# Block-sparse attention with an MLP behind it: dense query blocks left out of the sparse tiles, and window copies of the first chunk handed from ScalarE to GpSimd

## The chip, the cores and the metric

The kernel runs on one core of one Trainium2 chip. The metric is the time of one execution in device microseconds (us); the median of three runs of the kernel before is 761.54 us (760.61 to 762.57). A core has a TensorE (PE) for matmuls and transposes, a VectorE (DVE), a ScalarE (ACT), a GpSimd (POOL) and a SyncE (SP). SP and POOL issue nearly all the transfers here, and a transfer that is issued behind a waiting instruction waits with it, because each engine works through its instructions in the order of the program.

## The reference

Queries, keys and values have 4 batches, 8 heads, 768 positions and 64 dimensions. Positions form 24 blocks of 32. A query block sees its own and its two neighbour blocks, the first and the last block, and three sampled blocks; the first and the last query block see everything ("dense" blocks). The result of the attention, 3072 tokens of 512 numbers, goes through two weight matrices with a squared relu between them.

```python
mask = np.abs(blk_i - blk_j) <= window
mask = mask | (blk_i == 0) | (blk_j == 0) | (blk_i == n_blocks - 1) | (blk_j == n_blocks - 1)
for qb in range(n_blocks):
    for kb in sampled_blocks[qb]:
        mask[qb * block:(qb + 1) * block, kb * block:(kb + 1) * block] = True
scores = np.where(mask, scores, -1000000000.0)
...
attn = attn / (np.sum(attn, axis=-1, keepdims=True) + 1e-09)
return np.matmul(attn, v).astype(np.float32)
...
h = np.maximum(x @ w_in, 0.0)          # x 3072x512, w_in 512x2048
return (h * h @ w_out).astype(np.float32)
```

## The kernel before, in words

**Tiles and chunks.** 128 tokens of a batch (four query blocks) are a tile; there are 24 tiles `(b, t)` in `order`, and `k` is a tile's place in it. Three tiles form a chunk of 384 tokens, and there are eight chunks. The MLP of a chunk (`moe(c)`: `hidden` gives `ph` at L788, `project` gives `po` at L816 and L826) runs on PE while the attention of the chunks behind it is worked in between its steps. fp32 products are split into a rounded high part and a low part, and three products are summed, so each weight block has a high part, cast by ACT or DVE, and a low part, subtracted by POOL (`wi`/`wo` at L752 to L755, `WI` at L726 and L727).

**A half.** `Half(b, t, u)` is the attention of four heads of a tile. Each query block needs eight blocks of 32 keys: its window (`kn`, 96 columns) and a gathered set `KG` (first and last block and the three sampled ones, 160 columns). `scores` (L374) writes the scores `s` of the four query blocks into the four groups of 32 partitions: four groups, two column pieces, four heads, 32 matmuls. Then come `maxima` on DVE (L385), exponentials and a turn of the probabilities: for the first six tiles (`MOVED` = 6) by `exps` on ACT (L423), a transposition on PE (`pt`, L437) and copies (`pT`, L446 and L448); for the others by `turn_blocks`, 16 activations `pm` on ACT, each over a square of blocks (L413), and one DVE transposition (L418). `values` (L459) multiplies with the gathered values `V`, again 32 matmuls of 65 columns (64 values and a one for the sum), and `norm` writes `x`. In all this the dense blocks 0 and 23 go along like any other block, although their rows of `x` come from elsewhere.

**A whole.** `Whole(b, pr)` computes the two dense blocks for a pair of heads: scores `g` (L546), exponentials `pg` on ACT (L562), the turned `pTg`, and `pvg` (L604), for which 128 columns of `pTg` (two blocks of two heads) are multiplied in four pieces of 32 columns with each of six tiles of `vn`.

**The values of a tile.** `V[k]` is two tiles per `k`: the first and last block (`static`), a window of three neighbours (`window`) and three sampled blocks. They come by SP's DMAs (`load_static`, `load_window` L304, `load_sampled` L317), save for the second and third tile of the first chunk, whose windows and static blocks are copied from `vn` inside the chip (`copy_window` L217, `copy_static` L209).

**The start.** The first chunk has no MLP beside it. A `Stream` advances in ticks; every fifth tick another unit begins (four wholes, then six halves). Into the ticks go three lists: `fixed`, the copies given to ACT (6 static ones, then the 24 window copies of the third tile, `k` = 2); `moves`, the copies given to DVE (12 for the second half of the second tile); and the cuts. A cut turns a block of the float64 weights to fp32: POOL issues the load `craw` (L692), `AHEAD` = 5 cuts later ACT works on it (L708, L710), one cut later DVE (L719, L720), one later ACT and POOL split it if it stays resident (L726, L727). POOL's own list at the start is written out: gathered keys of two tiles, five loads of weights, 12 window copies, gathered keys of the third tile. `later` holds the key copies of the tiles behind (`copy_keys`, L263), of which a piece is issued at every tick or second tick.

The order on each engine is that of the code (a manual schedule); the pools add the waits.

Of the kernel before, what the change touches and what calls it, by code (L numbers as in the profile page):

```python
# [75 lines left out]
CUT_0 = (30, 5)  # L76
# [6 lines left out]
ON_ACT = 12  # L83
# [13 lines left out]
def tile_block_sparse_attention_moe(ctx: ExitStack, tc, kd, knd, qd, qgd, vd, vnd, samp, const, wcat, out):  # L97
# [59 lines left out]
    V = {0: [one.tile([P, 2, NJ, HW // 2], F32, name=f"V{c}") for c in range(2)]}  # L157
# [33 lines left out]
    def columns(src, us):  # L191

        return src.rearrange("... (u c) -> ... u c", u=2)[..., us, :]

    def load_static(k, u, eng=nc.sync):
        us = halves(k, u)
        if us is None:
            return
        n = 1 if k == 0 else NJ
        for i in range(us.start, us.stop):  # L200
            src = columns(vd[order[k][0], V_STATIC * BLK :], i)
            src = src.unsqueeze(1).broadcast_to([2 * BLK, n, HW // 2])
            eng.dma_start(values_of(k)[0][0 : 2 * BLK, i, 0:n], src)

    def copy_static(k, i, copy):

        src = V[0][0][0 : 2 * BLK, i, 0:1]
        dst = V[k][0][0 : 2 * BLK, i, 1 if k == 0 else 0 :]
        copy(dst, src.broadcast_to(list(dst.shape)))  # L209

    def copy_window(k, i, j, n, copy):
# [5 lines left out]
        copy(V[k][1][(1 + n) * BLK : (2 + n) * BLK, i, j], st["vn", b, i][r : r + BLK, blk // NJ])  # L217

    def load_vn(b, hf, eng=nc.sync, own=None):
# [3 lines left out]
        st["vn", b, hf] = vn  # L223

# [28 lines left out]
    def copy_keys(b, t, own=None):  # L253
# [3 lines left out]
        for u in range(2):  # L257
# [3 lines left out]
            for j in range(NJ):  # L261
# [6 lines left out]
    later = []  # L268

    def load_kg(b, t):  # L270
# [3 lines left out]
        for j in range(NJ):  # L274
# [11 lines left out]
    def load_window(k, u, eng=nc.sync):  # L286
# [5 lines left out]
        runs = []  # L292
        for j in range(NJ):
            c = centre(NJ * t + j)
            if runs and c == runs[-1][-1][1] + 1:
                runs[-1].append((j, c))
            else:
                runs.append([(j, c)])
        for run in runs:
            (j, c), n = run[0], len(run)  # L300
            for i in range(us.start, us.stop):
                src = vd[b, (c - 1) * BLK : (c + 1 + n) * BLK, i * HW // 2 : (i + 1) * HW // 2]
                src = bass.AP(src.tensor, src.offset, [[HW, 3 * BLK], [BLK * HW, n], [1, HW // 2]])
                eng.dma_start(VB[BLK:P, i, j : j + n], src)  # L304

    def load_sampled(k, u, eng, on):
# [6 lines left out]
        v4 = columns(vd[b], us).rearrange("(a p) u c -> p a u c", p=BLK)  # L313
        for j in range(NJ):
            for r in range(NRAND):
                dst = VB[0:BLK, us, j] if r == 2 else VA[(2 + r) * BLK : (3 + r) * BLK, us, j]
                eng.dma_start(dst.unsqueeze(1), v4[:, bass.ds(vals[NRAND * j + r], 1)])  # L317
# [6 lines left out]
    class Half:  # L324


        def __init__(self, b, t, u):
# [3 lines left out]
            self.name = f"{b}_{t}_{u}"  # L331

# [26 lines left out]
        def scores(self):  # L359
# [3 lines left out]
            for i in range(2):  # L363
                pr = 2 * u + i
                for piece in range(2):
                    for j in range(NJ):
                        c = centre(NJ * t + j)
                        for e in range(2):
# [3 lines left out]
                            else:  # L372
                                k, a, z = kg[r, j, :, pr, :], 0, S_WIN
                            nc.tensor.matmul(  # L374
                                self.sb[e][j * BLK : (j + 1) * BLK, i * NSLOT + a : i * NSLOT + z],
# [6 lines left out]
        def maxima(self):  # L382
            m = self.m = rot.tile([P, 2, 2], F32, tag="m", name=f"m{self.name}", bufs=4)
            for e in range(2):
                nc.vector.tensor_reduce(m[:, e], self.sb[e].rearrange("p (i c) -> p i c", i=2), axis=AX, op=ALU.max)  # L385
            self.p = rot.tile([P, 4, 2, NJ, BLK], F32, tag="p", name=f"p{self.name}", bufs=PBUFS)
            if not self.moved:
                nc.vector.tensor_scalar(m, m, -SCALE, None, op0=ALU.mult)
                return
            for e in range(2):  # L390
                nc.vector.tensor_tensor(  # L391
                    self.p[:, 2 * e : 2 * e + 2].rearrange("p h c a s -> p h (c a s)"),
                    self.sb[e].rearrange("p (i c) -> p i c", i=2),
                    m[:, e].unsqueeze(2).broadcast_to([P, 2, NSLOT]),
# [9 lines left out]
        def turn_blocks(self):  # L404
# [4 lines left out]
            for j in range(NJ):  # L409
                if j == 2:  # L410
                    self.next_keys()
                for a in range(NJ):
# [491 lines left out]
    for _ in range(AHEAD):  # L904
        cut_next()
# [107 lines left out]
```

## Time and profile before

| | |
|---|---|
| median of three runs | 761.54 us (760.61 to 762.57) |
| span of the profiled execution | 757.7 us, of which the other 3.8 us of the median lie around it |
| PE busy | 733.0 us (97% of the span) |
| PE weight loads (PEld) | 612.4 us (81%) |
| ACT busy | 539.4 us (71%) |
| POOL busy | 502.1 us (66%) |
| DVE busy | 500.2 us (66%) |
| HBM traffic | 126 GB/s over the span |

The profiled execution has no time of its own beyond its span; the median of the three runs is taken as its time, so that 3.8 us (761.5 less 757.7) lie outside the span. In the span the start (up to about 58 us, before the MLP begins) differs from the rest: there PE is well below full, and ACT, DVE and POOL take turns in a chain of small steps. In the rest PE runs almost without a gap. The views that the prediction shows are windows (busy time of each engine in a stretch), groups (one line and tile: count, busy time, mean of one), and timelines (start, duration, engine, line, operation, count, and in brackets the idle time before with what ended it).

### The profile page before, as it was taken

To read this page: it belongs to the slowest core of one execution; us is meant where nothing else is said; L and a number is where in the kernel's file an instruction comes from. 1 tells how busy PE (TensorE), PEld (TensorE's weight loads), DVE (VectorE), ACT (ScalarE), POOL (GpSimd) and SP (SyncE) were. 2 spreads that over 40 slices of the span, in tenths; PEclk is the share of its full clock that TensorE was granted. 3 is DMA by queue.
4 is the path that set the end of the run, shared out by engine and by line. 5 is a ranking of instruction groups with operands and counts; after the bars stand their busy time and mean duration, and the time that the engine had idled before them with its cause. 6 is when DMAs were issued, how large, how long until landed. Compare 5 with 4: busy or idle time off the path is not lost.

```text
span 757.7 us, 26295 instructions
## 1 busy us (share of the span) xinstructions
PE 733.0 (97%) x9832; PEld 612.4 (81%) x9832; DVE 500.2 (66%) x988; ACT 539.4 (71%) x1193; POOL 502.1 (66%) x636
## 2 busy tenths in 40 slices
PE   5779999999999999999999999999999999999997
PEld 2666777678888888888888888887888888888986
DVE  5785785658785756667777575666868666645452
ACT  5896877898876876689786767679876776733222
POOL 6963844237776675757777567666876575777885
PEclk9899999999999999999999999999999999999999
DMA  8776799644443436544434344654344352201001
GB/s 282 217 210 187 223 272 339 136 119 141 125 119 92 144 90 186 153 105 118 119 102 107 98 126 107 225 120 139 84 122 114 81 138 65 51 1 44 1 1 42
DMA packets 92434, 97.45 MB, mean 129 GB/s; under 512 B 14803, under 2 KB 79700, under 8 KB 92308
## 3 DMA queue, kind: packets, MB, share of 16 engines
q1 hardware_dynamic: 86324, 72.80, 36.6%
q0 software_dynamic: 5696, 22.58, 8.8%
q8 instruction: 78, 1.28, 0.7%
q14 instruction: 48, 0.39, 0.2%
q10 hardware_dynamic: 288, 0.39, 0.1%
HBM read 89.43 MB, written 6.29 MB: 126 GB/s over the span
## 4 chain that ended last, share of the span: by engine, by line
PE 84%; DMA 5%; ACT 5%; DVE 3%; issue 1%; SPq 1%; POOL 1%; ACTq 0%; POOLq 0%; DVEq 0%
PE ph L788 33%; PE po L826 30%; PE s L374 7%; PE pv L459 6%; DMA V<-in_v_dram 3%; PE po L816 3%; PE g L546 2%; PE pvg L604 2%; DMA KG<-in_k_dram 1%; PE pt L437 1%; PE xt L773 1%; DVE xl L777 1%; ACT V L209 1%; DMA kn<-in_kn_dram 1%; SPq L317 1%
## 5 line engine op out<-in xcount | busy, mean ns | idle before, releaser
L413 ACT ACTIVATE pm<-p 32x256 f32<-32x256 f32 x576 | 239.2, 415 | 13.2 <-DVE p L391 4.9
L788 PE MATMUL ph<-xh,wi 128*128 128x384 f32 x832 | 237.8, 347 | 0.0
L826 PE MATMUL po<-wo,gh 128*128 128x512 f32 x672 | 213.8, 399 | 0.0
L755 POOL TENSOR_TENSOR wi<-W,wi 128x512 fp32r<-128x512 f32 x104 | 142.2, 1367 | 66.8 <-DVE wi L754 35.2
L806 POOL TENSOR_TENSOR gl<-gf,gh 128x384 fp32r<-128x384 f32 x112 | 117.4, 1048 | 93.3 <-DVE gf L804 80.9
L755 POOL TENSOR_TENSOR wo<-WO,wo 128x512 fp32r<-128x512 f32 x112 | 145.8, 1301 | 49.5 <-DVE wo L754 48.6
L792 ACT ACTIVATE r<-ph 128x384 f32<-128x384 f32 x128 | 63.0, 492 | 161.6 <-PE ph L788 156.5
L804 DVE SCALAR_TENSOR_TENSOR gf<-ph,r 128x384 f32<-128x384 f32 x112 | 62.3, 556 | 150.7 <-ACT r L792 137.1
L788 PEld LDWEIGHTS ph<-xh,wi 128*128 128x128 f32 x832 | 150.4, 188 | 13.4 <-issue 7.4
L826 PEld LDWEIGHTS po<-wo,gh 128*128 128x128 f32 x672 | 123.5, 188 | 23.0 <-issue 2.8
L788 PE MATMUL ph<-xl,wi 128*128 128x384 f32 x416 | 141.4, 340 | 0.0
L826 PE MATMUL po<-wo,gl 128*128 128x512 f32 x336 | 133.1, 396 | 0.0
L754 DVE CAST wo<-WO 128x512 fp32r<-128x512 f32 x112 | 84.3, 753 | 0.0
L788 PEld LDWEIGHTS ph<-xl,wi 128*128 128x128 f32 x416 | 78.2, 188 | 6.9 <-issue 2.9
L826 PEld LDWEIGHTS po<-wo,gl 128*128 128x128 f32 x336 | 63.1, 188 | 15.7 <-POOL gl L806 1.0
L385 DVE TENSOR_REDUCE m<-s 128x2 f32<-128x512 f32 x96 | 61.6, 683 | 10.6 <-PE s L374 10.2
L799 ACT ACTIVATE gh<-r 128x384 fp32r<-128x384 f32 x112 | 59.0, 527 | 9.3 <-ACT r L792 0.4
L459 PEld LDWEIGHTS pv<-V,pT 128*32 128x32 f32 x3072 | 47.2, 109 | 18.9 <-issue 10.5
L459 PE MATMUL pv<-V,pT 128*32 128x65 f32 x3072 | 56.0, 221 | 4.4 <-ACT pT L446 2.3
L788 PE MATMUL ph<-xh,WI 128*128 128x384 f32 x192 | 54.4, 344 | 0.8 <-ACT xh L776 0.8
L374 PE MATMUL s<-KG,q 64*32 64x160 f32 x1536 | 51.3, 307 | 0.6 <-issue 0.3
L418 DVE STREAM_TRANSPOSE pT<-pm 128x1024 f32<-128x1024 f32 x36 | 44.6, 1238 | 4.9 <-ACT pm L413 4.7
(89 smaller groups left out, 933.9 us busy)
## 6 DMA issues: line engine op xcount, KB each, us to landing
craw<-in_w_dram POOLq DMA_DIRECT2D x32, 512.0 KB, 6.0
V<-in_v_dram SPq DMA_DIRECT2D x504, 32.5 KB, 1.8
KG<-in_k_dram SPq DMA_DIRECT2D x216, 64.0 KB, 2.0
V<-in_v_dram SPq DMA_DIRECT2D x28, 390.0 KB, 4.3
q<-in_q_dram SPq DMA_DIRECT2D x24, 256.0 KB, 3.6
out_dram<-ot SPq DMA_DIRECT2D x22, 256.0 KB, 2.6
V<-in_v_dram SPq DMA_DIRECT2D x16, 292.5 KB, 4.0
vn<-in_vn_dram SPq DMA_DIRECT2D x5, 780.0 KB, 6.2
```

The costliest lines, as they stand in the source:

```text
L374: nc.tensor.matmul(self.sb[e][j * BLK : (j + 1) * BLK, i * NSLOT + a : i * NSLOT + z], q[r, j, pr, :], k, start=True, stop=True,)
L385: nc.vector.tensor_reduce(m[:, e], self.sb[e].rearrange("p (i c) -> p i c", i=2), axis=AX, op=ALU.max)
L413: nc.scalar.activation(p[a * BLK : (a + 1) * BLK, j], x[j * BLK : (j + 1) * BLK, :, a], AF.Exp, scale=SCALE)
L459: nc.tensor.matmul(po[j * BLK : (j + 1) * BLK, h * VW : (h + 1) * VW], self.pT[:, j, 2 * e + i, c], v[:, self.u, j, hv : hv + VW], start=( ...
L754: nc.vector.tensor_copy(w[:, 0], src)
L755: nc.gpsimd.tensor_tensor(w[:, 1], src, w[:, 0], op=ALU.subtract)
L788: nc.tensor.matmul(ph[:, :TOK], w, x, start=(i == 0), stop=(i == len(steps) - 1))
L792: nc.scalar.activation(r, ph[:, :TOK], AF.Relu)
L799: nc.scalar.activation(gh, r, AF.Square)
L804: nc.vector.scalar_tensor_tensor(gf, ph[:, :TOK], 0.0, r, op0=ALU.max, op1=ALU.mult)
L806: nc.gpsimd.tensor_tensor(gl, gf, gh, op=ALU.subtract)
L826: nc.tensor.matmul(acc[c][u], g[:, at], w[:, k], start=(f == 0 and i == 0), stop=(f == NF - 1 and i == 2))
```

## The change

Six edits, in the diff below.

- **Dense blocks left out of the halves.** `groups(t)` lists the query blocks that a half works on: (2, 3, 1) in a batch's first tile, (0, 1, 2) in its last, all four elsewhere. In 16 of the 48 halves `s` and `pv` have 24 matmuls instead of 32, the exponentials and maxima 96 partitions instead of 128, `pm` 12 activations instead of 16, and a quarter of the sampled blocks is neither loaded nor copied. The block at group `g` is no longer block `g` in the first tile, so `norm` writes in two parts there.
- **`pvg` in 64 columns.** The layout of `QG` is changed in the host arrays, so that a head's two dense blocks lie side by side, and `Whole.values` has two pieces of 64 columns instead of four of 32.
- **Halves of `V` side by side.** In the first chunk a row of `V` holds both halves, so one DMA with rows of 2080 bytes brings what two rows of 1040 bytes did, and a window or a static block comes in one DMA.
- **Third tile's windows on POOL.** The 24 copies leave ACT's `fixed` and stand in POOL's list behind the fourth load of weights. That list is now: two loads, 12 window copies, a load, the third tile's keys, a load, 24 window copies, the fifth load.
- **Weights later.** `CUT_0` moves from tick 30 to 35, so five cuts instead of six begin in the first chunk, and the sixth follows in `moe(0)`.
- **Fourth tile's values later.** Its window and sampled loads go to a list `late`, of which one entry is issued every four ticks of `moe(0)`.

```diff
-CUT_0 = (30, 5)
+CUT_0 = (35, 5)
-ON_ACT = 12
+FIRST_LOADS, SECOND_LOADS, THIRD_LOADS = 2, 3, 4
+LATE = (0, 4)
...
-    V = {0: [one.tile([P, 2, NJ, HW // 2], F32, name=f"V{c}") for c in range(2)]}
+    V = {0: [one.tile([P, NJ, 2, HW // 2], F32, name=f"V{c}") for c in range(2)]}
...
+    def groups(t):
+        return (2, 3, 1) if t == 0 else tuple(range(NJ - 1 if t == NT - 1 else NJ))
...
-                    for j in range(NJ):
+                    for g, j in enumerate(self.js):
...
-                                self.sb[e][j * BLK : (j + 1) * BLK, i * NSLOT + a : i * NSLOT + z],
+                                self.sb[e][g * BLK : (g + 1) * BLK, i * NSLOT + a : i * NSLOT + z],
...
+                if g >= len(self.js):
+                    yield NJ
+                    continue
                 for a in range(NJ):
                     nc.scalar.activation(
-                        p[a * BLK : (a + 1) * BLK, j], x[j * BLK : (j + 1) * BLK, :, a], AF.Exp, scale=SCALE
+                        p[a * BLK : (a + 1) * BLK, g], x[g * BLK : (g + 1) * BLK, :, a], AF.Exp, scale=SCALE
                     )
...
-                        nc.tensor.transpose(pt[e][:, a : a + P], self.p[:, 2 * e + i, c], ident)
+                        nc.tensor.transpose(pt[e][:, a : a + n], self.p[:n, 2 * e + i, c], ident[:n, :n])
...
-            whole = {0: ((BLK, 2 * BLK), (2 * BLK, P)), NT - 1: ((0, P - BLK),)}
-            for at in (slice(*r) for r in whole.get(t, ((0, P),))):
-                nc.vector.tensor_tensor(x3[at], po3[at, :, 0:D], rec3[at], op=ALU.mult)
+            parts = ((2 * BLK, 0, 2 * BLK), (BLK, 2 * BLK, 3 * BLK)) if t == 0 else ((0, 0, at.stop),)
+            for to, a, z in parts:
+                nc.vector.tensor_tensor(x3[to : to + z - a], po3[a:z, :, 0:D], rec3[a:z], op=ALU.mult)
...
-                load_window(n, self.u)
-                load_sampled(n, self.u, nc.sync, SP)
+                if k == 0:
+                    late.append((load_window, n, self.u, nc.sync))
+                    late.append((load_sampled, n, self.u, nc.sync, SP))
+                else:
+                    load_window(n, self.u)
+                    load_sampled(n, self.u, nc.sync, SP)
...
-                for g in range(4):
-                    h = pr % 2 * 2 + g % 2
+                for e in range(2):
+                    h = pr % 2 * 2 + e
+                    a = kt * P + e * D
                     nc.tensor.matmul(
-                        po[g * BLK : (g + 1) * BLK, :VW],
-                        self.pT[:, a + g * BLK : a + (g + 1) * BLK],
+                        po[e * D : (e + 1) * D, :VW],
+                        self.pT[:, a : a + D],
...
-    for _ in range(AHEAD):
-        cut_next()
-    for k in range(1, UC):
-        if k == 1:
-            for f, *at in windows[k, 0]:
+    for i in range(AHEAD + 1):
+        if i == FIRST_LOADS:
+            for f, *at in windows[1, 0]:
                 f(*at, nc.gpsimd.tensor_copy)
+        if i == SECOND_LOADS:
             deque(copy_keys(0, 2, begin), 0)
+        if i == THIRD_LOADS:
+            for f, *at in windows[2, 0] + windows[2, 1]:
+                f(*at, nc.gpsimd.tensor_copy)
+        if i < AHEAD:
+            cut_next()
     fixed = [(copy_static, k, i) for k in range(UC) for i in range(2)]
-    fixed += windows[2, 0] + windows[2, 1][:ON_ACT]
-    moves = windows[1, 1] + windows[2, 1][ON_ACT:]
+    moves = windows[1, 1]
...
+            if c == 0 and late and now >= LATE[0] and (now - LATE[0]) % LATE[1] == 0:
+                f, *at = late.pop(0)
+                f(*at)
```

On POOL, behind the gathered keys of the first two tiles, the program before has all five loads in a row. `V_123` holds values of the second tile and `V_125` those of the third; `KG_407` and `KG_390` are the third tile's keys.

```order
L692 DMA craw_0_360<-in_w_dram 128x1024
L692 DMA craw_0_362<-in_w_dram 128x1024
L692 DMA craw_0_364<-in_w_dram 128x1024
L692 DMA craw_0_366<-in_w_dram 128x1024
L692 DMA craw_1_368<-in_w_dram 128x1024
L217 COPY V_123<-vn_0_133 32x260 x12
L231 TENSOR_LOAD idx
L284 COPY KG_407<-kn_0_126 128x4x2x64
```

In the changed program the same place begins so:

```order
L715 DMA craw_0_347<-in_w_dram 128x1024
L715 DMA craw_0_349<-in_w_dram 128x1024
L223 COPY V_123<-vn_0_132 32x260 x12
L715 DMA craw_0_363<-in_w_dram 128x1024
L241 TENSOR_LOAD idx
```

and, once the third tile's keys are copied, goes on:

```order
L715 DMA craw_0_417<-in_w_dram 128x1024
L223 COPY V_125<-vn_0_132 32x260 x12
L223 COPY V_125<-vn_1_136 32x260 x12
L715 DMA craw_1_443<-in_w_dram 128x1024
```

The fifth load now stands behind 36 window copies and the third tile's keys instead of ahead of them, and 24 copies are new on POOL.

On ACT, from the first half's exponentials to the second's (`p_0_0` to `p_1_0`), the program before has copies of `V_125` and a cut in between:

```order
L423 ACTIVATE p_0_0_668<-s_0_0_1_596,m_0_0_665 128x256 x2
L217 COPY V_125<-vn_1_137 32x260 x5
L446 COPY pT_0_0_815<-pt_0_0_0_786 128x4x4x32
L446 COPY pT_0_0_815<-pt_0_0_1_787 128x4x4x32
L423 ACTIVATE p_0_1_799<-s_0_1_0_690,m_0_1_796 128x256 x2
L423 ACTIVATE p_0_1_799<-s_0_1_1_691,m_0_1_796 128x256 x2
L217 COPY V_125<-vn_1_137 32x260
L708 ACTIVATE ct_827<-craw_0_360 128x512
L710 ACTIVATE craw_0_360<-craw_0_360,below 128x512
L217 COPY V_125<-vn_1_137 32x260 x4
L446 COPY pT_0_1_970<-pt_0_1_0_906 128x4x4x32
```

The changed program has there only the steps of the halves, on 96 rows:

```order
L439 ACTIVATE p_0_0_625<-s_0_0_1_575,m_0_0_622 96x256 x2
L464 COPY pT_0_0_745<-pt_0_0_0_718 128x4x3x32
L464 COPY pT_0_0_745<-pt_0_0_1_719 128x4x3x32
L439 ACTIVATE p_0_1_731<-s_0_1_0_644,m_0_1_728 96x256 x2
L439 ACTIVATE p_0_1_731<-s_0_1_1_645,m_0_1_728 96x256 x2
L464 COPY pT_0_1_844<-pt_0_1_0_820 128x4x3x32
```

The copies are gone from ACT and the first cut begins a half later, behind `p_1_0`.

On SP, behind the loads for the first three tiles, the program before loads the fourth tile's values (`V_78`, `V_79`) between the queries of two tiles:

```order
L242 DMA q_3_724<-in_q_dram 128x512
L304 DMA V_79<-in_v_dram 96x4x260
L231 TENSOR_LOAD idx
```

The changed program issues both queries first, and a window is the last thing ahead of `q_5`:

```order
L252 DMA q_3_670<-in_q_dram 128x512
L252 DMA q_4_890<-in_q_dram 128x512
L307 DMA V_79<-in_v_dram 96x4x260
L241 TENSOR_LOAD idx
```

The first half's values of the fourth tile now stand behind `q_4`, and the second half's 12 sampled loads behind `q_5`.

More of the change, by code (lines that the diff above doesn't have):

```diff
@@ L268, in tile_block_sparse_attention_moe @@
     later = []
+    late = []
     def load_kg(b, t):
@@ L291, in load_window @@
         VB = values_of(k)[1]
[L292 to L304, printed above, removed]
+        js = sorted(groups(t))
+        j, c, n = js[0], NJ * t + js[0], len(js)
+        src = columns(vd[b, (c - 1) * BLK : (c + 1 + n) * BLK], us)
+        src = bass.AP(src.tensor, src.offset, [[HW, 3 * BLK], [BLK * HW, n], [1, src.shape[-1]]])
+        eng.dma_start(places(VB, slice(BLK, P), slice(j, j + n), us), src)
     def load_sampled(k, u, eng, on):
@@ L331, in __init__ @@
             self.name = f"{b}_{t}_{u}"
+            self.js = groups(t)
+            self.rows = slice(0, len(self.js) * BLK)
         def run(self, bank, lag):
```

91 lines of the change are left out of this document (53 added, 38 removed).

## The prediction

> **What bounds the kernel now.** I read the page first, then busy time by stretch, then the timelines of ACT, POOL, DVE and PE in the start.
>
> ```profile
> span 757.7 us, 26295 instructions
> PE 84%; DMA 5%; ACT 5%; DVE 3%; issue 1%; SPq 1%; POOL 1%; ACTq 0%; POOLq 0%; DVEq 0%
> ```
>
> The chain of work that ended last is PE for 84% of the span. Windows cut at the start of the first chunk, in its middle, at the beginning of the MLP and at 168 us show where it is not (span of the window, then busy us of PE, PEld, DVE, ACT, POOL, then PE's granted clock, DMA share, GB/s):
>
> ```profile
> 10.33:34.04 23.71, 17.40 (x395) 12.24 (x402) 17.35 (x57) 21.07 (x42) 21.30 (x80) 0.86 0.89 259
> 34.04:58.20 24.16, 19.79 (x670) 15.92 (x655) 19.29 (x44) 23.61 (x50) 16.37 (x58) 0.93 0.71 203
> 62.00:168.00 106.00, 105.65 (x1328) 74.57 (x1316) 70.73 (x120) 87.07 (x175) 46.77 (x73) 1.00 0.73 211
> 168.00:700.00 532.00, 530.17 (x7161) 458.21 (x7155) 362.81 (x711) 390.77 (x897) 367.64 (x366) 1.00 0.42 112
> ```
>
> From 62 to 700 us PE idles 2.2 us of 638. There only fewer PE microseconds help, and work taken off ACT, POOL, DVE or DMA is worth nothing unless PE waited for it. In the start it is otherwise: ACT is busy 23.61 of 24.16 us, and PE idles 4.4 us in that window and 6.3 us in the one before. So I cost two things: how much earlier the MLP begins, and how many PE microseconds go later.
>
> **The start, ACT's side.** Groups of ACT from 10 to 58.2 us, and the copies and the last cut of its timeline:
>
> ```profile
> L217 ACT COPY V<-vn 32x260 f32<-32x260 f32 x24 | 9.7, 405 | 0.4
> ...
> 35.63 0.40 ACT L217 COPY V<-vn 32x260 f32<-32x260 f32 x1
> ...
> 43.64 0.41 ACT L217 COPY V<-vn 32x260 f32<-32x260 f32 x1
> 56.37 0.88 ACT L708 ACTIVATE WO<-craw 128x512 f32<-128x512 f32 x1
> 56.97 0.93 ACT L710 ACTIVATE craw<-craw,below 128x512 int32<-128x512 uint16 x1
> 58.20 1.56 ACT L776 CAST xh<-xt 128x512 fp32r<-128x512 f32 x3 [0.31 <-PE xt L773]
> ```
>
> The MLP begins with `xh` at 58.20. ACT loses 24 copies (9.7 us) and one cut (56.37 to 57.90, 1.5 us): 11.2 us. The floor of the gain is what lies in the second window, where ACT has no gaps: seven copies (those shown are the first and the last; 7 x 0.405 = 2.8) and the cut, 4.3 us. The 17 copies before lie in a window where ACT too had 2.6 us free and DVE and PE took turns with it, so part of their 6.9 us turns into waits for maxima and transpositions. PE's idle of both windows, 10.7 us, is a ceiling. POOL gives a nearer one:
>
> ```profile
> 20.28 2.62 POOL L692 DMA_DIRECT2D craw<-in_w_dram  x5
> 22.94 5.23 POOL L217 COPY V<-vn 32x260 f32<-32x260 f32 x12
> 28.23 0.61 POOL L284 COPY KG<-kn 128x512 f32<-128x512 f32 x1
> ...
> 31.86 4.82 POOL L263 COPY KG<-kn 128x64 f32 x24
> ...
> craw<-in_w_dram POOLq DMA_DIRECT2D x32, 512.0 KB, 6.0
> ```
>
> A load costs POOL 0.53, a window copy 0.436 (5.23 / 12), the third tile's keys 6.0 (28.23 to 31.86, and half of the 4.82). Three key copies fewer ahead of them let POOL begin at 19.7 instead of 20.28. Then two loads, 12 copies, a load, keys, a load and 24 copies: 19.7 + 4 x 0.53 + 36 x 0.436 + 6.0 = 43.5. There the fifth load is issued, which lands 6.0 later, at 49.5, and ACT cuts it (1.5) ahead of `xh`: 51.0 at the earliest, a gain of at most 7.2. Between 4.3 and 7.2 I take 6.0, nearer the ceiling, because PE's idle and the first window's copies speak for more than the floor. `xh` then comes at 52.2. The third tile's windows are in place at 43.5; its first `pv` stood at 52.75 and comes some five earlier, so they are in time by 4 us.
>
> **The start, POOL's side.** POOL must still bring the low halves of the first weights, and it has 10.5 us of copies more:
>
> ```profile
> 48.46 1.33 POOL L727 TENSOR_TENSOR WI<-ct,WI 128x512 fp32r<-128x512 f32 x1 [7.30 <-ACT WI L726]
> 50.30 1.10 POOL L263 COPY KG<-kn 128x64 f32 x6
> 51.89 2.72 POOL L263 COPY KG<-kn 128x64 f32 x9
> 55.08 2.14 POOL L263 COPY KG<-kn 128x64 f32 x6
> 60.37 1.27 POOL L755 TENSOR_TENSOR wi<-W,wi 128x512 fp32r<-128x512 f32 x1 [2.66 <-ACT wi L752]
> ...
> 64.47 0.50 PE L788 MATMUL ph<-xh,wi 128*128 128x384 f32 x2
> ...
> 52.56 0.70 DVE L719 SCALAR_TENSOR_TENSOR W<-W,craw 128x512 int32<-128x512 int32 x1
> 53.30 0.70 DVE L720 SCALAR_TENSOR_TENSOR W<-craw,W 128x512 int32<-128x512 int32 x1
> ```
>
> Before, POOL idled 7.30 and 2.66 us here. Now, from 44.0 (the fifth load issued), it has 48 key copies, five loads, one `WI` (1.33) and one `wi` (1.27): 5.3 us besides the keys. At 0.18 a copy (1.10 / 6) `wi` is done at 44.0 + 5.3 + 8.6 = 57.9. At 0.284 (1.10 + 2.72 + 2.14 over 21 copies) it is done at 62.9. The slower pace belongs to stretches in which DVE works at L719 and L720; nine copies took 2.72 there instead of 1.6. PE used the first low half at about 64.4, which six microseconds earlier is 58.4. So the give-back lies between 0 and 4.5 us. I take the middle, 2.2.
>
> The Trainium skill, page "SBUF — State Buffer", section "Who interferes with whom", speaks against handing ACT's copies to POOL: DVE and GpSimd share a pair of ports as an exclusive lock, a DVE instruction with two SBUF inputs blocks a GpSimd instruction that reads SBUF, and ACT never waits. The trace agrees in kind (2.72 instead of 1.6 us beside L719 and L720). By that rule the two or three pairs L719/L720 beside the window copies would each hold them 1.4 us, the give-back would be 7.3 to 8.7, and the sum about 762, which is the third rival below.
>
> **PE after the start.** What the halves and wholes cost PE:
>
> ```profile
> 180.13 0.89 PE L604 MATMUL pvg<-vn,pTg 128*32 128x65 f32 x48
> ...
> 182.55 1.12 PE L459 MATMUL pv<-V,pT 128*32 128x65 f32 x64
> 183.59 0.40 PE L374 MATMUL s<-kn,q 64*32 64x96 f32 x16
> 183.78 0.48 PE L374 MATMUL s<-KG,q 64*32 64x160 f32 x16
> 184.06 0.37 PE L374 MATMUL s<-kn,q 64*32 64x96 f32 x16
> ...
> 46.41 1.09 PE L437 MATMUL pt<-ident,p 128*128 128x128 f32 x8
> 47.43 0.40 PE L374 MATMUL s<-kn,q 64*32 64x96 f32 x16
> ```
>
> From start to start `pv` takes 1.04 us for 64 instructions of 65 columns, 16 ns each, while a transposition of full width takes 1.02 / 8 = 128 ns for 128 columns, 1.0 ns a column. Sixteen rounds of four narrow instructions at 65 ns are also 1.0 ns a column: four groups of 32 run side by side and a round lasts as long as one. `s` says the same: 16 instructions of 96 columns take 0.19, 16 of 160 take 0.28. Leaving out one group of four makes rounds of three, not fewer rounds. So I put `s` and `pv` of the 16 halves at 0; the bounds are 0 and a quarter of `s` (twice 0.19 + 0.28) and `pv` (1.04) in 16 halves, 7.9 us. `pvg` goes from 12 rounds of four to 12 rounds of two: 0, with half of 0.89 x 16 = 7.1 as the upper bound and, for weights of 64 columns that load less well behind the matmuls, a loss of some microseconds as the lower. The two short halves of the first batch's last tile save 8 x 32 columns of `pt` each, 0.5 us together on PE (those of the first tile lie in the start, which is counted already).
>
> ACT's relief could reach PE where PE waits for it:
>
> ```profile
> L413 ACT ACTIVATE pm<-p 32x256 f32<-32x256 f32 x576 | 239.2, 415 | 13.2 <-DVE p L391 4.9
> PE s L374 <- ACT pg L562: 1.5, 2, 0.8
> ...
> 342.21 0.35 PE L374 MATMUL s<-kn,q 64*32 64x96 f32 x2
> 343.32 0.31 PE L374 MATMUL s<-kn,q 64*32 64x96 f32 x7 [0.77 <-ACT pg L562]
> ```
>
> Twelve of the 16 short halves are turned on ACT and lose four `pm` each: 48 x 0.415 = 19.9 us of ACT's time, nearly all hidden by PE. There are two waits for `pg`, which stands behind `pm` on ACT; from 342.21 to 343.32 `s` is held 1.1 us, so two cost about 2.2. Fewer `pm` ahead take perhaps a third of that, 0.7 us. The bounds are 0 and 2.2. With `pt` that is 1.2.
>
> **Transfers.** The first chunk's `V` comes in fewer DMAs; no `pv` there waits for a DMA, so 0. The fourth tile's values are later on SP:
>
> ```profile
> 49.87 7.00 SPq L317 DMA_DIRECT2D V<-in_v_dram  x12
> V<-in_v_dram SPq DMA_DIRECT2D x504, 32.5 KB, 1.8
> 71.83 0.40 PE L374 MATMUL s<-kn,q 64*32 64x96 f32 x16
> ...
> 89.46 1.12 PE L459 MATMUL pv<-V,pT 128*32 128x65 f32 x64
> ```
>
> The second half's 12 sampled loads are behind `q_5`, which waits for the scores of the fourth tile's second half (71.83 before, about 68 then); 7.0 us to issue and 1.8 to land give 77, before its `pv` at 89.5 - 5 = 84.5. Cost 0; if issue is doubled, 84, still in time. The postponed cut comes back as 1.5 us of ACT and 1.4 of DVE after 62 us, where ACT is 82% busy and PE full: 0, up to 1.5 if `gp` ahead of L816 waits for it.
>
> **The sum.** Against the profiled span: -6.0 (MLP begins earlier) + 2.2 (POOL late) - 1.2 (`pt`, and PE's waits for ACT) = -5.0; 757.7 becomes 752.7. The median lies 3.8 above the span, which stays: 756.5. A measurement of this kernel tells about 0.3% (2.3 us) from no change: faster is under 759.3, slower over 763.8.
>
> **Rivals.**
> - *POOL keeps its pace* and `wi` is done by 58: the start gives 7.0, nothing is given back, and 2 us of `pt` and waits go: -9.0, 752.5. For it: the V copies ran at 0.436 with DVE 73% busy around them. Against it: 48 key copies share the stretch with L719 and L720. Chance 0.2.
> - *PE's time goes with instructions, not columns*: the quarter of `s` and `pv` and the half of `pvg` count, up to 15.0 us on top of the forecast: 741 to 748. Against it stand 0.19 and 0.28 for equal counts. Chance 0.05.
> - *POOL gives the start back.* `wi`'s low half lands between 63.3 and 67.9: the give-back is 4.9 to 9.5 against 7.2 gained, the net within 2.3 of zero: about 761. The mechanism: two or three pairs L719/L720 (0.70 + 0.70 each) fall beside the 24 copies, 33.0 to 43.5, and hold them, 2.8 to 4.2 us on top of 62.9. For it: nine keys beside such a pair took 1.1 longer. Against it: cuts then begin a half later, so one or two pairs are likelier there. A loss on `pvg` of 4 us would end here too. Chance 0.14.
> - *Slower*: DVE's other work in that stretch (maxima, its 12 window copies) holds POOL too, and the 24 copies stretch from 0.436 to over 0.65, so that `wi`, 62.9 by the slow pace of the keys, is done 5 us later still. It decides from 67.9 on, where PE's wait in the first `ph` is 9.5 us, the 7.2 gained and the 2.3 of the bound: 764 to 767. Against it: that is a pace that no row shows for `V` copies. Chance 0.08.
> - *The forecast*: 0.53.
>
> **How the numbers follow.** Forecast and its two neighbours hold 0.87: 752.5, 756.5 and 761. 751.0 to 761.5 leaves out PE's case, the slower case and the far end of the even one, under 0.2. Faster: 0.53 + 0.2 + 0.05, less 0.02 for the part of the forecast that ends above 759.3 (give-back 4.5) = 0.76. Same: 0.14 + 0.02 = 0.16. Slower: 0.08.
>
> **What would show it.** In the changed profile: `xh` at 51 to 53; on ACT no `V<-vn` rows; on POOL 36 window copies ending at 43 to 46, and `wi`'s first low half at 58 to 63 with PE waiting for POOL there; `s` and `pv` of short halves as long as before with x12 and x48; `pvg` x24 still at 0.8; PE busy in the rest within 2 us. The prediction is wrong if `xh` comes after 54 or before 50, if `pvg` moves by more than 0.1, or if PE waits for POOL more than 5 us.

## The result and the profile after

The changed kernel takes 754.34 us (median of four runs, 753.22 to 754.79), the kernel before 761.44 on the same chip: a ratio of 0.9908, 95% interval 0.9884 to 0.9932. The forecast was 756.5 in a range of 751.0 to 761.5. The time fits, but it came together from other places than the forecast had it, as the profile and the runs below show.

The head of the page of the changed kernel:

```profile
span 752.2 us, 24183 instructions
PE 728.1 (97%) x8936; PEld 608.7 (81%) x8936; DVE 498.2 (66%) x988; ACT 508.8 (68%) x1121; POOL 508.7 (68%) x648
```

PE has 896 matmuls fewer (the trace counts two for each `s`, `pv` and `pvg` matmul of the code: 32 fewer in each of 16 halves, 24 fewer in each of 16 wholes) and only 4.9 us of busy time less, so most of the matmuls that went cost nothing, as forecast. The span is 5.5 us shorter. (The first profile of before was one of its quicker executions, with a span 3.8 under the median, while the four of the changed kernel lie 1.7 to 1.8 under their times; in a later group before's eighteen times run from 757.4 to 765.7 and the changed kernel's six from 753.6 to 755.2.)

Windows of the changed kernel that answer to those of before (columns as there):

```profile
10.33:34.04 23.71, 19.03 (x467) 13.98 (x465) 19.73 (x62) 16.28 (x31) 20.06 (x78) 1.00 0.81 237
34.04:52.00 17.96, 13.36 (x421) 10.65 (x422) 15.28 (x38) 15.46 (x34) 16.80 (x45) 1.00 0.68 181
56.00:162.00 106.00, 104.13 (x1158) 72.72 (x1158) 73.26 (x121) 84.77 (x169) 48.18 (x86) 0.98 0.77 227
```

ACT, busy for 23.61 of 24.16 us in the second window before, now idles 2.5 of 18. POOL, at 16.8 of 18, is now the busiest. Where the time went is read at two marks on PE. The first is the first `po`, with which PE's full stretch begins. Before:

```profile
66.20 2.31 PE L816 MATMUL po<-WO,gp 128*128 128x512 f32 x5
```

After, with what PE waited for ahead of it:

```profile
54.60 0.45 PE L811 MATMUL ph<-xh,WI 128*128 128x384 f32 x1 [1.66 <-ACT xh L799]
56.58 0.62 PE L811 MATMUL ph<-xh,WI 128*128 128x384 f32 x2 [0.57 <-POOL WI L750]
62.11 0.62 PE L811 MATMUL ph<-xh,wi 128*128 128x384 f32 x2 [0.33 <-POOL wi L778]
63.96 2.31 PE L839 MATMUL po<-WO,gp 128*128 128x512 f32 x5
```

So the whole start is worth 2.2 us there. ACT's and POOL's rows say why it is not more:

```profile
51.78 0.69 ACT L731 ACTIVATE WO<-craw 128x512 f32<-128x512 f32 x1 [1.25 <-DMA craw<-in_w_dram]
53.02 1.53 ACT L799 CAST xh<-xt 128x512 fp32r<-128x512 f32 x3
```

```profile
20.95 1.05 POOL L715 DMA_DIRECT2D craw<-in_w_dram  x2
22.04 5.23 POOL L223 COPY V<-vn 32x260 f32<-32x260 f32 x12
34.26 12.47 POOL L223 COPY V<-vn 32x260 f32<-32x260 f32 x24
46.68 0.53 POOL L715 DMA_DIRECT2D craw<-in_w_dram  x1
55.27 1.26 POOL L750 TENSOR_TENSOR WI<-ct,WI 128x512 fp32r<-128x512 f32 x1
60.77 1.29 POOL L778 TENSOR_TENSOR wi<-W,wi 128x512 fp32r<-128x512 f32 x1
```

`xh` comes at 53.02, 5.2 us earlier. But POOL's first low half is done only at 62.06, so PE reaches its first `po` 2.2 earlier, and 3.0 of the 5.2 are given back. In before that low half was done at 61.64, hardly earlier, but there PE asked for it only at 64.47. The fourteen profiles of this document bear it out: from `xh` to the first `po` takes 8.0 us in seven of them, and 8.9 to 11.5 in the other seven, which are those with all 24 copies on POOL and the key copies where the changed kernel has them.

The second mark is the full stretch. From the third chunk's transposition to the eighth's, first before and then after:

```profile
248.28:680.74 432.46, 430.63 (x5870) 372.26 (x5869) 292.03 (x569) 321.28 (x737) 295.97 (x290) 1.00 0.43 113
```

```profile
245.78:675.15 429.37, 429.28 (x5357) 371.37 (x5356) 288.68 (x569) 304.39 (x697) 297.23 (x290) 1.00 0.41 107
```

The same work takes 3.1 us less here: PE's idle time falls from 1.8 to 0.1, and its busy time by 1.35. Groups of PE from 170 to 690 us, before and after, name both:

```profile
L374 PE MATMUL s<-KG,q 64*32 64x160 f32 x1056 | 34.4, 301 | 0.3 <-issue 0.3
L374 PE MATMUL s<-kn,q 64*32 64x96 f32 x1056 | 26.2, 249 | 1.5 <-ACT pg L562 1.5
```

```profile
L380 PE MATMUL s<-KG,q 64*32 64x160 f32 x976 | 32.9, 300 | 0.0
L380 PE MATMUL s<-kn,q 64*32 64x96 f32 x976 | 25.9, 249 | 0.1
L627 PE MATMUL pvg<-vn,pTg 128*64 128x65 f32 x288 | 11.0, 226 | 0.0
```

The waits of `s` for ACT are nearly gone, and `s` itself is shorter by 1.8; the ten short halves in this stretch make 1.0 of that (0.10 each). A short half in the timeline:

```profile
108.70 0.38 PE L380 MATMUL s<-kn,q 64*32 64x96 f32 x12
108.89 0.47 PE L380 MATMUL s<-KG,q 64*32 64x160 f32 x12
109.16 0.36 PE L380 MATMUL s<-kn,q 64*32 64x96 f32 x12
109.32 0.48 PE L380 MATMUL s<-KG,q 64*32 64x160 f32 x12
109.74 0.70 PE L839 MATMUL po<-WO,gp 128*128 128x512 f32 x1
```

Its pieces begin 0.19, 0.27 and 0.16 us apart, as those of a full half, so a round is not shorter; only the last piece ends earlier, and the block takes 1.04 us (108.70 to 109.74) instead of 1.14.

### The profile page after: what moved, and what is told of

Its sections match the earlier page's. It is cut to its first block, busy times and chain, and to the rows that moved or that the text cites. A ratio compares the mean times of both kernels' runs of the same rounds, so it can differ in the third digit from the quotient of the medians.

```text
span 752.2 us, 24183 instructions
## 1 busy us (share of the span) xinstructions
PE 728.1 (97%) x8936; PEld 608.7 (81%) x8936; DVE 498.2 (66%) x988; ACT 508.8 (68%) x1121; POOL 508.7 (68%) x648
## 4 chain that ended last, share of the span: by engine, by line
PE 86%; DVE 5%; ACT 4%; issue 2%; DMA 1%; POOL 1%; ACTq 0%; POOLq 0%; DVEq 0%
PE ph L811 34%; PE po L849 31%; PE s L380 6%; PE pv L477 6%; PE po L839 4%; PE g L569 2%; PE pvg L627 2%; DMA kn<-in_kn_dram 1%; PE xt L796 1%; DVE m L392 1%; PE pt L454 1%; ACT p L439 1%; POOL KG L273 1%; ACT craw L733 1%; DVE WO L743 1%
## 5 line engine op out<-in xcount | busy, mean ns | idle before, releaser
L425 ACT ACTIVATE pm<-p 32x256 f32<-32x256 f32 x528 | 219.2, 415 | 15.6 <-DVE p L400 8.2
L392 DVE TENSOR_REDUCE m<-s 128x2 f32<-128x512 f32 (+1 forms) x96 | 61.5, 681 | 8.9 <-PE s L380 8.5
L380 PE MATMUL s<-KG,q 64*32 64x160 f32 x1408 | 48.4, 302 | 0.6 <-ACT KG L295 0.6
L777 DVE CAST wi<-W 128x512 fp32r<-128x512 f32 x91 | 47.4, 521 | 0.0
```

Source lines behind the costliest of these rows:

```text
L380: nc.tensor.matmul(self.sb[e][g * BLK : (g + 1) * BLK, i * NSLOT + a : i * NSLOT + z], q[r, j, pr, :], k, start=True, stop=True,)
L392: nc.vector.tensor_reduce(m[at, e], self.sb[e][at].rearrange("p (i c) -> p i c", i=2), axis=AX, op=ALU.max)
L425: nc.scalar.activation(p[a * BLK : (a + 1) * BLK, g], x[g * BLK : (g + 1) * BLK, :, a], AF.Exp, scale=SCALE)
L777: nc.vector.tensor_copy(w[:, 0], src)
```

## The experiments

All comparisons are with the kernel before, run beside each group. Four runs were made in each of three groups, each group on another chip, so medians are compared within a group and ratios between groups.

**The changed kernel again, and the short blocks by themselves.**

> The changed kernel as it is, as the measure for the other three of this group and with the kernel before beside it on the same chip. The profiled execution of before has a span 3.8 us under its median, those of the changed kernel lie 1.8 under theirs. Theory (the profile of before was a quick one): before's runs here have spans near 759.7, the two kernels differ by 7 us in time, and the changed one's profile again shows the TensorE clock falling to about 0.5 from 58 to 61 us. Rival (the fall of the clock is an accident of that one execution): it is not there again, and the first po begins some 1.5 us earlier.

Measured: 754.15, ratio 0.9905 (0.9873 to 0.9937); before 760.64. The spans of its executions are again 1.8 under their times, those of before 1.8 too, so the 3.8 of the first profile was that one execution's. The window from 58 to 60 us in the first profile of the changed kernel and in this one:

```profile
58.00:60.00 2.00, 2.00 (x20) 1.51 (x10) 1.31 (x3) 0.00 (x0) 2.00 (x10) 0.50 0.70 256
```

```profile
58.00:60.00 2.00, 2.00 (x70) 1.63 (x69) 0.65 (x2) 0.00 (x0) 2.00 (x11) 1.00 0.69 252
```

The granted clock had fallen to 0.50 in the first and stayed at 1.00 here. In this execution it fell elsewhere, from 45.4 to 48.8 us:

```profile
46.00:48.00 2.00, 1.82 (x11) 1.32 (x9) 1.81 (x3) 0.99 (x3) 1.96 (x6) 0.50 0.52 81
```

So the place of the fall is an accident of one execution, as the rival had it. It did not cost what the rival said: the first `po` began at 63.74 here and at 63.96 there, since PE waits for POOL's `wi` in both.

> The changed kernel with the dense query blocks worked in the halves again (all four groups, 32 matmuls, 16 pm); all else stays. From the two traces: s of a short half takes 1.04 instead of 1.14 us (14 halves, 1.4 us), pt 0.4, waits of s behind pm on ACT 2.5 to 3. Theory (these three are the edit's worth): 3.5 to 4.5 us slower than the changed kernel, about 758.3. Rival (the waits go for another reason, the earlier start): 1.8 slower, about 756. Rival (the term as forecast): 1.2 slower, 755.5.

```diff
     def groups(t):
-        return (2, 3, 1) if t == 0 else tuple(range(NJ - 1 if t == NT - 1 else NJ))
+        return tuple(range(NJ))
...
```

`load_window` and `norm` were put back with it. Measured: 759.68, ratio 0.999 (0.9961 to 1.0019): with every edit but this one, nothing of the gain is left that can be told. More than any theory said: 5.5 us over the changed kernel. The waits of `s` for `pg` are back to 1.5 us in two places, the first `po` comes 1.3 later (65.07), the way from there to the third chunk takes 1.0 longer, and the stretch from the third to the eighth chunk 2.7 longer:

```profile
247.80:679.80 432.00, 430.49 (x5678) 372.68 (x5677) 291.19 (x569) 321.37 (x737) 296.45 (x290) 1.00 0.41 114
```

> The kernel before with one edit alone, the dense query blocks left out of the halves; the first chunk's copies, cuts, V layout and loads stay as before. The kernel with all edits but this one measured 0.999 of before, and the one with all of them 0.9905. Theory (this edit carries nearly all of the gain): 0.991 to 0.994 of before, 4.5 to 7 us, and the first po no earlier than 1.5 us before 66.2. Rival (as forecast: this edit is worth 1.2 us and the start the rest): 0.998. Rival (the parts need each other, since ACT's relief in the start comes from both): 0.995 to 0.997.

The diff is that of the front for `groups`, `scores`, `maxima`, `turn`, `turn_blocks`, `copies`, `values`, `norm` and the loops over `sorted(groups(t))`, put into the kernel before; nothing else. Measured: 753.6, ratio 0.9932 (0.9918 to 0.9945). This edit alone brings what all six bring, as far as the intervals tell (0.9873 to 0.9937 there). The stretch from the third to the eighth chunk takes 429.5, as in the changed kernel. Part of the gain lies in the start, against the expectation: the first `po` begins at 63.53 with `xh` at 55.5 and the 24 copies still on ACT:

```profile
63.53 2.74 PE L835 MATMUL po<-WO,gp 128*128 128x512 f32 x6
```

**What the copies' move is worth.**

> The changed kernel with the third tile's 24 window copies back on ACT (in its list of fixed copies); all else stays. Theory (what the move wins at xh is mostly given back to POOL): xh comes 4 to 5 us later than in the changed kernel, at 57 to 58, but wi_1's low half is done before PE asks for it, the clock stays full, and the first po begins only 0.5 to 1.5 later (64.5 to 65.5): 755 to 756. Rival (the move carries the gain): time goes back by 4 to 6 us, to 758.5 to 760.

```diff
         if i == THIRD_LOADS:
-            for f, *at in windows[2, 0] + windows[2, 1]:
-                f(*at, nc.gpsimd.tensor_copy)
+            pass
...
+    fixed += windows[2, 0] + windows[2, 1]
```

Measured: 755.68, ratio 0.9924 (0.9893 to 0.9954). The time is 1.5 over the changed kernel of the same group, as the theory had it, not the rival's 4 to 6; the first `po` is 2.0 later, a little more than the theory's 0.5 to 1.5:

```profile
65.73 2.74 PE L839 MATMUL po<-WO,gp 128*128 128x512 f32 x6
```

> The changed kernel with the fourth and fifth tile's key copies later on POOL: they begin at tick 46 of the start instead of 25, and the fifth tile's come in the MLP, so that WI's and wi_1's low halves stand ahead of 45 and 24 of them. Theory (POOL's order sets the give-back): WI's low half is done by 52, wi_1's by 58.5, PE does not wait for POOL, the clock stays near full, and the first po begins 2 to 3 us earlier, at 61 to 62: 751.5 to 752.5. Rival (the fall of the clock comes anyway, since PE still waits for xh and xl): under 1 us gained, 753.5 or more.

```diff
-        if now % KEYS_N == 0 and later and next(later[0], True):
-            later.pop(0)
+        if now >= KEYS_AT and fed < KEYS_PIECES and later:   # KEYS_AT, KEYS_PIECES = 46, 8
+            fed += 1
+            if next(later[0], True):
+                later.pop(0)
```

Measured: 753.72, ratio 0.9904 (0.987 to 0.9939); not to be told from the changed kernel's 754.15. The first step of the theory is shown: `wi`'s first low half is done at 58.0 instead of 61.8, and the first `po` begins 1.8 earlier. But the second chunk's MLP begins only 0.6 earlier, and the next wait is visible at once; PE, ACT and POOL:

```profile
61.95 2.74 PE L840 MATMUL po<-WO,gp 128*128 128x512 f32 x6
...
65.91 0.62 PE L812 MATMUL ph<-xh,wi 128*128 128x384 f32 x2 [0.74 <-POOL wi L779]
...
63.87 0.62 ACT L776 CAST wi<-W 128x512 fp32r<-128x512 f32 x1 [1.54 <-DVE WO L744]
...
64.58 1.27 POOL L779 TENSOR_TENSOR wi<-W,wi 128x512 fp32r<-128x512 f32 x1 [2.33 <-ACT wi L776]
```

The second weight's low half now waits for ACT's cast, which waits for DVE's work on a cut. In the changed kernel's second profile the matmul that waits here begins at 66.67, so of the lead of 1.8 us 0.8 is left at 65.91. There the chain of cuts (load, ACT, DVE, ACT, POOL) sets the pace, and a PE that is there earlier waits in it.

> The changed kernel with the cuts beginning at tick 30 again, so that the sixth stands in the first chunk. Theory (POOL's order sets when the first ph can go on, not ACT): xh comes up to 1.5 us later, but wi_1's low half and the first po move by less than 0.5: 754 to 754.5. Rival (what ACT does ahead of xh is on the path to the end): 1 to 1.5 slower, 755.5.

```diff
-CUT_0 = (35, 5)
+CUT_0 = (30, 5)
```

Measured: 757.29, ratio 0.9971 (0.9954 to 0.9988), 2.5 and 3.1 us over the nearest kernels of its group (754.81 and 754.2); neither theory had that. The profile, of an execution of 755.63, has the first `po` at 65.24, 1.5 later than in the changed kernel's second profile; what makes up the rest is not shown. ACT's rows tell how the 1.5 arise:

```profile
50.85 0.66 ACT L731 ACTIVATE WO<-craw 128x512 f32<-128x512 f32 x1 [1.33 <-DMA craw<-in_w_dram]
51.42 0.74 ACT L733 ACTIVATE craw<-craw,below 128x512 int32<-128x512 uint16 x1
52.06 1.05 ACT L464 COPY pT<-pt 128x512 f32<-128x512 f32 x2
55.03 0.67 ACT L731 ACTIVATE WO<-craw 128x512 f32<-128x512 f32 x1 [1.92 <-DMA craw<-in_w_dram]
```

POOL issues the fifth load only after the 24 copies. A cut that begins a half earlier then stands on ACT ahead of the last `pT`, waits 1.33 for that load with `pT` behind it, and the sixth waits 1.92 with `xh` behind it. So with the copies on POOL the cuts have to come later; at tick 30 the kernel loses.

**Smaller parts.**

> The changed kernel, in which each short half keeps four more pm activations on ACT, on the free quarter of its tile (they read scores of a used block, and nothing reads what they write). So PE's s and pv are short, and ACT is loaded as before. Theory (about half of the edit's steady gain is ACT's: s no longer waits behind pm): s of short halves stays at 1.04, the waits of s at 340 and 515 us go back from 1.5 to about 2.2 us and one of 1.9 comes back near 372; 2 to 2.5 us slower than the changed kernel, about 756.5. Rival (the waits went because the first chunk ends earlier): not slower by more than 0.5.

```diff
                 if g >= len(self.js):
-                    yield NJ
+                    for a in range(NJ):
+                        nc.scalar.activation(
+                            p[a * BLK : (a + 1) * BLK, g], x[0:BLK, :, a], AF.Exp, scale=SCALE)
+                        yield 1
                     continue
```

Measured: 754.81, ratio 0.9949 (0.9936 to 0.9963), 0.6 over the group's nearest (754.2). `s` of short halves stays at 1.04. The two waits come back by half:

```profile
340.12 0.31 PE L380 MATMUL s<-kn,q 64*32 64x96 f32 x7 [0.41 <-ACT pg L589]
```

From the start of `s` to the next matmul behind it, these two halves take 2.24 us each in before, 1.88 and 1.89 here, and 1.52 and 1.51 in the changed kernel. The third wait, near 372, does not come back; it is absent with all blocks too, so the short blocks are not needed for that. In the third to eighth chunk the four `pm` are worth 0.8 us, not 2 to 2.5; the rest of what went there did not come from them.

> The changed kernel with pvg in four pieces of 32 columns again (in the new order of the columns). The traces show 0.85 us with two pieces of 64 and 0.82 with four of 32. Theory (wider weights cost 0.03 us each and nothing else): 16 x 0.03 = 0.5 us faster than the changed kernel, 753.6, which five rounds hardly tell. Rival (fewer instructions relieve PE's queue in the start, where pv waits for nothing visible): 1 to 2 slower.

The edit is four pieces of 32 columns in `Whole.values` (`h = pr % 2 * 2 + g // 2`). Measured: 754.2, ratio 0.9937 (0.9924 to 0.9951): not to be told from the changed kernel. The trace agrees with the theory's term: a `pvg` took 0.82 again instead of 0.85.

> The changed kernel with the fourth tile's values loaded at once again, ahead of the queries of the fifth and sixth tile on SP, not from the list of late loads. Theory (SP has time either way): no difference, 753.9 to 754.4. Rival (these loads take bandwidth from the weights' loads in the start, for which ACT waited 1.25 us): 0.5 to 1.5 slower.

The edit takes `late` out of `loads`. Measured: 753.9, ratio 0.992 (0.9893 to 0.9948): no difference, as the theory had it.

**A second look at before, and two tries at better versions.**

> The kernel before, with a second profiled execution. Its first profile began the MLP (xt) at 57.5 us with 2.1 us of a wait for nothing visible in the start and a clock of 0.86 and 0.93 there; the kernel with short blocks alone, whose start is otherwise the same, began at 54.8 with a clock of 1.0. Theory (two of these three microseconds are differences between executions, not of the edit): here xt comes between 55 and 57, the waits for nothing visible stand at other instructions, and the steady part from the third chunk to the eighth takes 432.5 us again. Rival (the start of before is always as slow as in the first profile): xt at 57.5 again.

Measured: 760.5, ratio 1.0019 (0.9992 to 1.0047). The theory falls for the start: `xt` came at 57.1 again, and the wait for nothing visible stands at the same instruction again (below). The steady part took 432.6 again, as it said. So the start of before was later than that with short blocks in both of its profiles. The clock is not ruled out as part of the cause: in the windows from 10.33 to 34.04 and on to 58.20 it was 0.86 and 0.93 in the first profile of before, 0.90 and 0.96 in this one, and 1.00 in both with short blocks alone.

> The kernel before with short blocks and with the cuts beginning at tick 35, copies on ACT as before: one cut fewer ahead of xh, and POOL has time. Theory (the MLP's beginning is given back to the cuts that come after it): xh 1 to 1.5 us earlier than with short blocks alone (54 to 54.5), the second chunk's MLP no more than 0.5 earlier: 753.2 to 753.6, where short blocks alone measured 753.6. Rival (ACT ahead of xh is the bound to the end): 752.2.

Measured: 753.06, ratio 0.9911 (0.9875 to 0.9946), the lowest median of all, but within the intervals of short blocks alone and of the changed kernel. In its one profile the first `po` begins at 61.81, 1.7 before that of short blocks alone, and the second chunk's MLP 1.2 before, so the theory's "no more than 0.5" failed there. Of these 1.7, up to 1.25 need not be the edit's: the two waits for nothing visible in the start (shown below) add up to 1.27 here and to 2.52 with short blocks alone. Five rounds do not settle whether the gain lasts.

> The changed kernel with later key copies (as in the run with keys later) and only 12 of the third tile's 24 window copies on POOL, the other 12 on ACT, which idled 5 us between 23 and 34. POOL's fifth load then comes 6 us earlier, at about 40.5, so ACT does not wait for it ahead of xh. Theory (each engine's part fits its gaps): xh at 51 to 52.5, first po at 60 to 61.5, of which the cuts' chain after it gives back more than half: 752.5 to 753.3. Rival (the chain of cuts in the first MLP sets the second chunk's time whatever the start does): 753.5 to 754, no different from the changed kernel.

```diff
-            for f, *at in windows[2, 0] + windows[2, 1]:
+            for f, *at in windows[2, 0]:
...
+    fixed += windows[2, 1]
```

Measured: 754.16, ratio 0.9921 (0.9892 to 0.9951): no gain, and the mechanism expected was not seen. The first `po` begins at 66.26, since PE lost 3.6 us in the start to a wait that belongs to no engine:

```profile
34.77 0.49 PE L478 MATMUL pv<-V,pT 128*32 128x65 f32 x7 [3.62 <-issue]
```

## Why the prediction was right, and where it was not

The time lies in the range and the sign is right. That the sum on the span fits so closely (-5.0 forecast, -5.5 measured) is luck: up to the first `po` the change gave 2.2 instead of 3.8, behind it 3.3 instead of 1.2, and the two misses cancel. One edit carried the gain that the text gave to the others.

- **MLP begins earlier, -6.0.** The sum for `xh` was nearly right in the first profile: 53.02 instead of 52.2, -5.2. In the second it came at 54.83, -3.4, behind the 54 that the prediction names as a sign of being wrong. In the first, POOL was at the fifth load at 46.7, not 43.5: it began at 20.95, because a load of keys landed later, and 24 copies took 12.47 (0.52 each), not 10.5. The load then set `xh`, as the ceiling said: ACT waited 1.25 for it.
- **Give-back, +2.2 between 0 and 4.5.** It was 3.0 in the first profile and 0.9 in the second. `wi` done at 62.06 lies in the forecast's 57.9 to 62.9, near the slow end, though by another route: the keys kept about 0.2 a copy and the window copies took 0.52. The Trainium skill, page "SBUF — State Buffer", section "Who interferes with whom", has a DVE instruction with two SBUF inputs contend with a GpSimd instruction that reads SBUF. The trace agrees: the five of the 24 copies that lie beside L742 and L743 took 0.76 to 0.78 us, the other 19 about 0.40. So 24 copies that would take 10.5 at 0.436 took 12.47; the price here was 2 us of 12, not enough for the third rival.
- **The start's net, -3.8, is the first term that was mis-sized.** At the first `po` it was 2.2 and 2.5 in the two profiles. What was too large is the 6.0, taken "nearer the ceiling": relief of ACT counts only up to the next of several bounds (the fifth load, POOL's low halves, the chain of cuts), and the text priced the first two and not the third. The runs put the other edits lower still: all of them without the short blocks measured 0.999 of before, with the first `po` 0.7 to 1.1 earlier than in the two profiles of before, and short blocks alone reached it at 63.53. So the copies' move, `pvg`, the V layout, the late loads and the later cuts together add nothing that can be told on top of the short blocks, although within the changed kernel taking the copies' move back costs 1.5 us.
- **Short blocks on PE at 0 and ACT's relief at 0.7, with `pt` 1.2 in all.** This is the second term that was mis-sized, on the other side: -3.3 between the first `po` and the end in the first profile. `s` was worth 0.10 per short half, not 0 (12 undisturbed ones, 1.2); `pv` 0.01; `pt` 0.4 of the 0.5 forecast. The 0.7 for fewer `pm` was sized rightly: with the four `pm` kept, 0.8 comes back. But PE's idle time in the steady stretch fell by 1.7, and so about half of what the waits gave up is not the `pm`'s; where it comes from is open. (DVE has 3.4 us less to do in that stretch, and still has with the `pm` kept; whether that counts was not tried.) The rule behind the zero held: 12 instructions took nearly the time of 16.
- **`pvg` at 0.** It took 0.85 instead of 0.82, 0.5 us in 16: inside the bounds, and not to be told in the time.
- **The first chunk's own short halves** were said to be "counted already" with the start. That was wrong as far as the profiles go: with the copies still on ACT, the kernel with short blocks alone had its first `po` 2.3 to 2.7 earlier. How is argued below, not shown, and one profile speaks against a fixed amount: the changed kernel with the copies back on ACT has short halves too, and its first `po` (65.73) is hardly before that of before. Its waits for nothing visible add up to 4.87 us (1.70, 2.28 and 0.89), those of short blocks alone to 2.52. In the start, then, what an edit does and what these waits do is not separated.
- **Late values and V layout at 0.** The late loads cost nothing that the rounds can tell; the layout was not tried alone.
- **The offset of 3.8** between span and median was one execution's; it is 1.8. The forecast's -5.0 on the span stands against -5.5 and -5.9 (752.2 less 757.7, and 751.9 against 757.7), and against -7.1 and -6.5 in the medians; the 0.6 to 1.6 us between them stand in no profile.

## What to carry to other kernels

Relief of the busiest engine in a start-up stage is worth only what the next chain leaves. Take the bounds at the mark where the bound engine runs full (here the first `po`), not where the relieved engine finishes. Edits that move work to another engine must be tried without the edits beside them: here the plain removal of needless work gave the whole gain, and the moves around it added nothing that can be told, one of them costing 2.5 to 3 us without its partner. Add up the waits for nothing visible in each profile before a mark in the start is put down to an edit. A profile's span and the median of other runs are joined only by an offset from runs that have both.

## What was not expected of the hardware

PE's waits for nothing visible in the start are not random. Counted in the traces, those above 0.25 us inside a run of one kind of matmul stand at the same counts of matmuls from the program's beginning, in kernels whose instructions there differ: behind the 347th in both profiles of before, in short blocks alone and with later cuts; behind the 598th and the 724th in both profiles of the changed kernel and with the late loads undone; others behind the 471st or 472nd and the 846th or 847th. The steps are 122 to 126 matmuls. (A few records can be missing from a trace, so a count can be off by some.) In order: before (second profile), short blocks alone, the changed kernel (second profile).

```profile
30.35 0.65 PE L604 MATMUL pvg<-vn,pTg 128*32 128x65 f32 x13 [2.69 <-issue]
```

```profile
30.41 0.28 PE L380 MATMUL s<-kn,q 64*32 64x96 f32 x3 [1.28 <-issue]
34.96 0.51 PE L380 MATMUL s<-KG,q 64*32 64x160 f32 x16 [1.24 <-issue]
```

```profile
39.73 0.41 PE L477 MATMUL pv<-V,pT 128*32 128x65 f32 x10 [1.32 <-issue]
44.99 0.57 PE L477 MATMUL pv<-V,pT 128*32 128x65 f32 x20 [1.88 <-issue]
```

Each costs 0.3 to 2.7 us; the 3.62 of the run with split copies stands behind the 345th. That PE's instructions arrive in pieces of such a size, late while the data's transfers fill the queues (DMA share 0.7 to 0.9 there), would fit; no run shows it. It might also explain the short blocks' gain in the start: in before the piece ends inside `pvg`, ahead of the first `pt` on the path (2.69 us), and with short blocks in `s` behind it (1.28). But short blocks have a second such wait (1.24), and the two add up to nearly the same, so only their place could make the difference; that is not shown either.

The fall of the clock to 0.50 lasted 3.41 us in the first profile of the changed kernel, from 57.84 to 61.25, and in the 3.41 us ahead of it PE was busy for 2.15. The Trainium skill, page "TensorE: Matmul & The Clock Gate", section "What's actually happening", names such a fall after an idle window of about 3.4 us. The trace agrees with the length and not with the idleness: PE was busy for 63% of the stretch, and its longest gap there was 0.6 us. In the second profile the same kernel fell at 45.4 instead, and four of the other kernels (copies on ACT, short blocks alone, `pm` kept, late loads undone) not at all before the end of their work.
